# Weight loads of the expert stage from Pool's queue, and the token split on ScalarE and VectorE

## The chip, the cores and the metric

One core of a Trainium2 chip. The time is that of the device, from start to end of one launch, in microseconds (us); of several launches the median is given. The engines of a core run their own instruction lists side by side and meet at semaphores: TensorE (PE: matrix products; PEld is its loading of weights), VectorE (DVE), ScalarE (ACT), GpSimd (POOL) and SyncE (SP). SP, ACT and POOL can also issue DMA transfers; a queue named SPq or POOLq in the profile is the list of such issues on that engine. In this kernel SP issues plain loads and transposes, POOL issues gathers and scatters through lists of row numbers.

## The reference

Three parts follow each other. `x` (8 x 8 x 512 x 64) and a small state attend to each other; the result is laid out as 4352 tokens of 512 numbers. Each token goes to the one of eight experts whose embedding it is nearest to, and the output is a feed-forward layer over all tokens:

```
xread = softmax(x @ state.T) @ state;  sread = softmax(state @ x.T) @ x     # 8 batches, 8 heads
x     = tokens of (xread, sread)                                            # 4352 x 512
e     = argmax(normalized(x) @ normalized(expert_emb).T)                    # one of 8 for each token
out   = gate * (relu(x[e] @ w1[e]) @ w2[e])                                 # w1 512x1024, w2 1024x512
h     = out @ w_in;  y = (max(h, 0) + alpha * min(h, 0)) @ w_out            # w_in 512x2048, w_out 2048x512
```

All in float32. The kernel keeps that precision by splitting each number into two float16 parts, `hi` and `lo`, and adding three products: hi x hi, lo x hi and hi x lo.

## The kernel before, in words

The attention stage takes the first 142 us of the profiled execution, the expert stage goes to about 595 us, and the feed-forward stage (`ffn`) fills the rest. The change lies in the expert stage (`moe`).

The tokens are sorted by expert and cut into tiles of 128, called slots; `step(s)` does the work of one slot. For each slot `mm1` multiplies the tokens by `w1h` and `w1l` (24 products), `relu` splits the result into `hs`, and `mm2` multiplies that by `w2h` and `w2l` (24 products, one slot behind `mm1`: TensorE's order is mm1(s), mm2(s-1), mm1(s+1), mm2(s)). Both need their operand with the tokens along the free axis, so two transfers transpose on the way: `xs` to `xTt` (line 1043) and `hs` to `hT` (line 1060). Both are issued by SP. hT(s) has from the end of the split of mm1(s) to the end of mm1(s+1); xTt(s) is issued two steps ahead.

The tokens of slot s+4 are gathered by Pool (`g_load`, line 1037) into `xg`. Two steps before their use `x_prep` (line 1040) scales them and splits them into `xs`; before, Pool does this in three instructions a slot (`split_pool`, lines 141 to 143). Pool also scatters the finished rows (`y_out`, line 1085), after one small copy (line 1081).

The weights of one expert at a time are in float16 in SBUF. Where the next slot has another expert, `swap` converts the waiting float32 copy (`st1`, `st2`) to float16 on ACT and DVE (`convert`, lines 130, 133, 188) and then loads the next expert's weights into that copy, in four transfers of 512 KB (line 1103). Which slots these are is known only at run time: a table says it, and an engine that takes part reads its flag and branches (lines 1097, 1099, 1107). `sq` squares the loaded copy on ACT (line 164), which gives its scale. An expert's w1 and w2 are changed in neighbouring steps.

In the same steps the feed-forward weights are loaded too, 1 MB at a time (`d_load`, lines 1110 to 1117): 16 of them, one in every second step or so, each decoded by three instructions on DVE (lines 149 to 151) behind it. The first expert's weights are loaded elsewhere, in the attention stage (`w_load`, line 698), from SP; the change leaves that.

What one engine executes is in the order in which the program is written. In one step the order is: mm1, mm2 of the slot before, relu and hT, the change of w1, the feed-forward work left from the step before (with `d_load`), the squares of st2, `x_prep`, `y_top`, the change of w2, the squares of st1, `y_out`, the next gather. A compiler sets the semaphores; an engine that waits holds all that is written behind it.

Of the kernel before, what the change touches and what calls it, by code (L numbers as in the profile page):

```python
# [14 lines left out]
ALU = mybir.AluOpType  # L15
AX = mybir.AxisListType
ET = mybir.EngineType
# [5 lines left out]
def tile_attn_moe_ffn(ctx, tc, x, xt, state, statet, embt, tau, w1, w2, w_in, w_out, alpha, out):  # L23


    nc = tc.nc
    B, S, DM = x.shape
    D, NS = state.shape[2], statet.shape[3]
    H = DM // D
    E, _, FE = w1.shape  # L30
# [84 lines left out]
    def flag(row, s, engines, mx):  # L115
        return nc.values_load(
            tab[0:1, row, s:s + 1], engines=engines, min_val=0, max_val=mx,
            skip_runtime_bounds_check_because="the table is computed in this launch within these bounds",
        )
# [9 lines left out]
    def split_hi(hi, src, sc):  # L129
        nc.scalar.activation(out=hi, in_=src, func=AF.Copy, scale=sc)  # L130

    def split_lo(lo, hi, src, sc):
        nc.vector.scalar_tensor_tensor(out=lo, in0=src, scalar=sc, in1=hi, op0=ALU.mult, op1=ALU.subtract)  # L133

    def split(hi, lo, src, sc):
        split_hi(hi, src, sc)
        split_lo(lo, hi, src, sc)

    def split_pool(hi, lo, src, sc):

        nc.gpsimd.tensor_tensor(src, src, sc.to_broadcast([128, src.shape[1]]), ALU.mult)
        nc.gpsimd.tensor_copy(hi, src)
        nc.gpsimd.tensor_tensor(lo, src, hi, ALU.subtract)

    def decode_ops(dst, d):

# [38 lines left out]
    def convert(i):  # L185
        src, hi, lo = W[i]
        if i == 1:
            nc.vector.tensor_scalar(hi[:, 3, :], src[:, 3, :], a_w[i][:, 0:1], None, ALU.mult)
        for c in range(4):
            if c < 3 or i != 1:  # L190
                split_hi(hi[:, c, :], src[:, c, :], a_w[i])
            split_lo(lo[:, c, :], hi[:, c, :], src[:, c, :], a_w[i])
        nc.vector.reciprocal(inv_w[i], a_w[i])
# [816 lines left out]
    def moe(st, winh, winl, wf, yq, yps, scp, pm, tables, order, gates):  # L1010
# [4 lines left out]
        def ring(pool, n, shape, dt, name):  # L1015
            ts = [pool.tile(shape, dt, name=f"{name}{i}", tag=f"{name}{i}", bufs=1) for i in range(n)]
            return [ts[i % n] for i in range(MS + 1)]

        xg = ring(mp, 5, [128, XW], F32, "xg")
# [19 lines left out]

        def x_prep(s):  # L1040
            xs = xs_[s]
            split_pool(xs[:, 0:DM], xs[:, DM:], xg[s][:, 0:DM], xg[s][:, DM:DM + 1])
            nc.sync.dma_start_transpose(out=xTt[s], in_=xs)

        def mm1(s):
# [50 lines left out]
        def swap(i, s, wv, stg):  # L1096
            with tc.If(flag(0, s, (ET.Activation, ET.DVE), 1) > 0):
                convert(i)
            with tc.If(flag(1, s, (ET.SP,), 1) > 0):
                nxt = flag(2, s, (ET.SP,), E - 1)  # L1100
                n = stg.shape[1] // 4
                for c in range(4):
                    nc.sync.dma_start(stg[:, c * n:(c + 1) * n, :],
                                      wv[bass.ds(nxt, 1), :, c * n:(c + 1) * n, :].rearrange("e p k f -> p (e k) f"))

        def sq(i, s):
            with tc.If(flag(1, s, (ET.Activation,), 1) > 0):
# [2 lines left out]
        def d_load(c):  # L1110
            d64[c] = mp.tile([128, 1024, 2], I32, tag="d64", bufs=1, name="d64")
            if c < 8:
                src = w_in32[(c // 2) * 128:(c // 2 + 1) * 128, (c % 2) * 2048:(c % 2 + 1) * 2048]
                nc.sync.dma_start(d64[c].rearrange("p a b -> p (a b)"), src)
            else:
                src = w_out32[(c - 8) * 256:(c - 7) * 256, :].rearrange("(k p) n -> p k n", p=128)
                nc.sync.dma_start(d64[c].rearrange("p (k a) b -> p k (a b)", k=2), src)

        def d_parts(c):
            cs = slice((c % 8) * 1024, (c % 8 + 1) * 1024)  # L1120
            ops = decode_ops(wf[:, cs], d64[c])
            if c < 15:
                ops.append(lambda: d_load(c + 1))
            return ops
# [6 lines left out]
        d64, work = {}, {s: [] for s in range(MS)}  # L1131
# [20 lines left out]
        x, xs = xg[ES], xs_[ES]  # L1152
        split(xs[:, 0:DM], xs[:, DM:], x[:, 0:DM], x[:, DM:DM + 1])
        nc.sync.dma_start_transpose(out=xTt[ES], in_=xs)
        swap(0, ES, w1v, st1)
        squares(1)
        x_prep(ES + 1)
        order(le, mp, pos, ids)
        for i in range(2):
            nc.gpsimd.memset(ys_[i][:, 2 * DM:YW], 0.0)  # L1160
        y_top(0)
        y_out(0)
        d_load(0)

        left = []

        def step(s):
# [19 lines left out]
            if s + 1 < MS:  # L1187
                swap(0, s + 1, w1v, st1)
# [5 lines left out]
            if s + 2 < MS:  # L1194
                x_prep(s + 2)
            y_top(s - 1)
            swap(1, s, w2v, st2)
            sq(0, s)
            y_out(s - 1, fill)
# [378 lines left out]
```

## Time and profile before

| | |
|---|---|
| three runs | 1281.7, 1278.25, 1269.78 us; median 1278.25 |
| the profiled execution's own time | 1269.9 us |
| its span | 1268.2 us |
| mean granted clock of TensorE | 0.986 |
| busy in the span: PE, DVE, ACT, POOL | 94%, 63%, 45%, 25% |
| chain that ended last | PE 53% of the span, DMA 1%, the others under 0.5% |

The profile is one execution. Its span is cut into stages below; the granted clock is the share of full speed that TensorE was given. In a row of groups the columns are: line, engine, operation, what it writes and reads, shape, count, then busy time in us and the mean of one in ns, then the idle time of the engine just before them and what ended it. A row of waits names the engine and the line that waited, for whom, the total in us, how often, and the longest. A row of a timeline gives the start in us, the duration in us, and in brackets what the engine waited for before.

### The profile page before, as it was taken

The page shows a single profiled execution, that of the slowest core. Times are in us where ns is not written, and L with a number is a line of the kernel's source. Part 1 is how long each engine was busy: PE and PEld are TensorE (multiplying, and loading weights), DVE is VectorE, ACT ScalarE, POOL GpSimd, SP SyncE. Part 2 cuts the span into 40 slices and gives each one's busy share as a digit, 9 for nine tenths or more (in the row PEclk, how much of TensorE's full clock was granted, in tenths as well). Part 3 has the DMA queues.
Part 4 walks back from the last instruction along what each step waited for, and adds up shares of the span by engine and source line. Part 5 has one row for each costly group of instructions (what it writes and reads, how often), then busy time and mean ns, then how long its engine had stood idle before and what let it go on. Part 6 is the DMA issues. An engine that isn't in the chain of part 4 may idle for free.

```text
span 1268.2 us, 21066 instructions
## 1 busy us (share of the span) xinstructions
PE 1194.9 (94%) x7520; PEld 680.0 (54%) x7520; DVE 794.8 (63%) x1648; ACT 565.1 (45%) x1045; POOL 323.3 (25%) x389
## 2 busy tenths in 40 slices
PE   8998899998778899998999999999999999999997
PEld 5555444443333344443446666666666666666664
DVE  5899676586676577755997546445454554555443
ACT  5986422264563545542544334333333433334343
POOL 2113355535345446453202011020100201001010
PEclk9999999998998999998999999999999999999999
DMA  9998678998999999984011010100101002000000
GB/s 286 289 295 257 174 169 203 188 234 202 225 255 209 219 227 234 207 195 88 12 18 51 1 42 26 35 34 1 43 26 34 34 1 51 18 18 35 1 26 26
DMA packets 221648, 148.48 MB, mean 117 GB/s; under 512 B 174014, under 2 KB 190526, under 8 KB 220480
## 3 DMA queue, kind: packets, MB, share of 16 engines
q1 hardware_dynamic: 210976, 117.30, 38.5%
q0 software_dynamic: 10240, 29.49, 8.1%
q8 instruction: 61, 1.00, 0.3%
q14 instruction: 83, 0.68, 0.2%
q10 hardware_dynamic: 288, 0.02, 0.0%
HBM read 80.13 MB, written 28.40 MB: 86 GB/s over the span
## 4 chain that ended last, share of the span: by engine, by line
PE 53%; DMA 1%; DVE 0%; issue 0%; ACT 0%; POOLq 0%; DVEq 0%
PE bk L1394 27%; PE pm L1448 12%; PE bk L1448 9%; PE bk L1410 2%; PE pm L1410 1%; DMA hT<-hs 1%; PE yp L1065 1%; DMA out_dram<-arena,fr 0%; POOLq L1574 0%; DVE ys L133 0%; DVE arena L1454 0%; DVE ym L1072 0%; ACT arena L1399 0%; ACT ys L130 0%; ACT arena L1367 0%
## 5 line engine op out<-in xcount | busy, mean ns | idle before, releaser
L1394 PE MATMUL bk<-woh,arena 128*128 128x512 f16 x1088 | 399.8, 379 | 0.0
L1394 PEld LDWEIGHTS <-arena 128*128 128x128 f16 x1632 | 158.1, 98 | 100.2
L1394 PE MATMUL bk<-wol,arena 128*128 128x512 f16 x544 | 206.2, 379 | 0.0
L1454 DVE SCALAR_TENSOR_TENSOR arena<-bk,sg,arena 128x256 f32<-128x256 f32 (+1 forms) x128 | 59.8, 467 | 215.4 <-PE bk L1448 215.3
L1456 ACT ACTIVATE arena<-pm,sg 128x256 f32<-128x256 f32 (+1 forms) x192 | 88.2, 460 | 195.3 <-PE pm L1448 193.8
L1065 PE MATMUL yp<-w2h,hT 128*128 128x512 f16 x576 | 140.6, 400 | 33.0 <-DMA hT<-hs 32.0
L1065 PEld LDWEIGHTS <-hT 128*128 128x128 f16 x864 | 83.3, 100 | 142.1 <-DMA hT<-hs 39.0
L1367 ACT CAST arena<-arena 128x512 f16<-128x512 f32 (+1 forms) x144 | 85.1, 591 | 157.7 <-DVE arena L1372 156.2
L1052 PEld LDWEIGHTS <-xTt 128*128 128x128 f16 x864 | 84.4, 98 | 122.1 <-DMA xTt<-xs 13.6
L1052 PE MATMUL hp<-w1h,xTt 128*128 128x512 f16 x576 | 133.3, 383 | 15.5 <-DMA xTt<-xs 9.8
L1283 POOL DMA_INDIRECT gt<-gate_d,fr x34 | 36.7, 1078 | 392.7 <-DMA fr<-y_nat 326.3
L1448 PEld LDWEIGHTS <-wS 128*128 128x128 f16 x1152 | 108.3, 98 | 50.6 <-issue 0.2
L1448 PEld LDWEIGHTS <-winh 128*128 128x128 f16 x1024 | 98.6, 98 | 64.5 <-issue 0.8
L1372 DVE SCALAR_TENSOR_TENSOR arena<-arena,alpha_sb 128x512 f32<-128x512 f32 (+1 forms) x144 | 103.0, 716 | 3.2 <-ACT arena L1414 3.2
L1371 DVE TENSOR_TENSOR arena<-arena 128x512 f16<-128x512 f32 (+1 forms) x144 | 94.3, 660 | 16.1 <-ACT arena L1367 13.6
L130 ACT ACTIVATE ys<-yp,ym 128x512 f16<-128x512 f32 x38 | 26.0, 684 | 171.4 <-DVE ym L1074 154.7
L1448 PE MATMUL pm<-ysum,wS 128*128 128x256 f16 (+1 forms) x768 | 99.6, 266 | 0.1
L1085 POOL DMA_INDIRECT y_nat<-ys,pos x38 | 39.4, 1038 | 211.6 <-issue 146.4
L1294 POOL DMA_INDIRECT out_dram<-arena,fr x34 | 34.9, 1025 | 203.9 <-ACT arena L1399 143.7
L1448 PE MATMUL bk<-yT,winh 128*128 128x256 f16 (+1 forms) x512 | 86.5, 266 | 0.0
L1052 PE MATMUL hp<-w1l,xTt 128*128 128x512 f16 x288 | 68.2, 379 | 0.0
L1065 PE MATMUL yp<-w2l,hT 128*128 128x512 f16 x288 | 68.0, 378 | 0.0
(315 smaller groups left out, 1860.5 us busy)
## 6 DMA issues: line engine op xcount, KB each, us to landing
st<-in_w_dram SPq DMA_DIRECT2D x64, 512.0 KB
X<-in_x_dram SPq DMA_DIRECT2D x32, 256.0 KB
d<-in_w_in_dram SPq DMA_DIRECT2D x8, 1024.0 KB
d<-in_w_out_dram SPq DMA_DIRECT2D x8, 1024.0 KB
xs_all<-xrow SPq DMA_DIRECT2D x7, 1056.0 KB
xT<-in_xt_dram SPq DMA_DIRECT2D x7, 1024.0 KB
xs_all<-xrow SPq DMA_DIRECT2D x2, 528.0 KB
xT<-in_xt_dram SPq DMA_DIRECT2D x2, 512.0 KB
```

The source lines that it names most:

```text
L1052: nc.tensor.matmul(hp[s][c], lhsT=xTt[s][:, q + k, :], rhs=wt[:, k, c * 512:(c + 1) * 512], start=(i == 0 and k == 0), stop=(i == 2 and k ...
L1065: nc.tensor.matmul(yp[s], lhsT=hT[s][:, q + k, :], rhs=wt[:, k, :], start=(i == 0 and k == 0), stop=(i == 2 and k == KE - 1))
L1085: nc.gpsimd.indirect_dma_start(out=y_nat[:], out_offset=bass.IndirectOffsetOnAxis(ap=pos[:, s:s + 1], axis=0), in_=ys[:].bitcast(I32), in_ ...
L1283: nc.gpsimd.indirect_dma_start(out=gt[g][:, t:t + 1], out_offset=None, in_=gate_d[:], in_offset=bass.IndirectOffsetOnAxis(ap=fr[g][:, t, 1 ...
L1367: nc.scalar.copy(slot[G[g, m]][:, 0, 0:n], h)
L1371: tt(d[:, 1, 0:n], h, d[:, 0, 0:n], sub)
L1372: return [lambda: nc.vector.scalar_tensor_tensor(h, in0=h, scalar=alpha_sb[:, m:m + 1], in1=h, op0=ALU.mult, op1=ALU.max), hi, lo]
L1394: nc.tensor.matmul(ps, lhsT=slot[G[g, m]][:, lg, t * 128:(t + 1) * 128], rhs=wo[lw][:, m, :], start=(m == order[0] and i == 0), stop=(m == ...
L1410: nc.tensor.matmul(ps, lhsT=wi[l][:, k, m * 128:(m + 1) * 128], rhs=yT[0][:, y + k, :], start=(n == 0), stop=(n == 11))
L1448: nc.tensor.matmul(ps, lhsT=a, rhs=b, start=(i in (1, 2, 5) and j == 0), stop=(j == len(ops) - 1), skip_group_check=True)
L1454: nc.vector.scalar_tensor_tensor(d, in0=ps, scalar=sc, in1=d, op0=ALU.mult, op1=add)
L1456: nc.scalar.activation(out=d, in_=ps, func=AF.Copy, scale=sc)
```

## The change

`split_pool` is gone. `x_prep` calls `split`, the pair that line 130 (ACT) and line 133 (DVE) of the other conversions use. The flag, the branch and the four loads of `swap` move from SP to Pool, and so do the 16 feed-forward loads. Line numbers after the change are 6 lower behind line 143.

```diff
-    def split_pool(hi, lo, src, sc):
-        nc.gpsimd.tensor_tensor(src, src, sc.to_broadcast([128, src.shape[1]]), ALU.mult)
-        nc.gpsimd.tensor_copy(hi, src)
-        nc.gpsimd.tensor_tensor(lo, src, hi, ALU.subtract)
...
         def x_prep(s):
             xs = xs_[s]
-            split_pool(xs[:, 0:DM], xs[:, DM:], xg[s][:, 0:DM], xg[s][:, DM:DM + 1])
+            split(xs[:, 0:DM], xs[:, DM:], xg[s][:, 0:DM], xg[s][:, DM:DM + 1])
             nc.sync.dma_start_transpose(out=xTt[s], in_=xs)
...
-            with tc.If(flag(1, s, (ET.SP,), 1) > 0):
-                nxt = flag(2, s, (ET.SP,), E - 1)
+            with tc.If(flag(1, s, (ET.Pool,), 1) > 0):
+                nxt = flag(2, s, (ET.Pool,), E - 1)
                 n = stg.shape[1] // 4
                 for c in range(4):
-                    nc.sync.dma_start(stg[:, c * n:(c + 1) * n, :],
+                    nc.gpsimd.dma_start(stg[:, c * n:(c + 1) * n, :],
...
-                nc.sync.dma_start(d64[c].rearrange("p a b -> p (a b)"), src)
+                nc.gpsimd.dma_start(d64[c].rearrange("p a b -> p (a b)"), src)
...
-                nc.sync.dma_start(d64[c].rearrange("p (k a) b -> p k (a b)", k=2), src)
+                nc.gpsimd.dma_start(d64[c].rearrange("p (k a) b -> p k (a b)", k=2), src)
```

SP's list in one early step of the expert stage, before: `st` is the float32 copy of expert weights, `tab` the table of flags, `d` a feed-forward load; ISA rows set up the row number of a load.

```order
L1060 DMA_TRANSPOSE hT_2248<-hs_2246 128x16x128
L1092 UNCONDITIONAL_BRANCH
L1097 UNCONDITIONAL_BRANCH
L116 TENSOR_LOAD tab
L1099 COMPARE_AND_BRANCH
L116 TENSOR_LOAD tab
L1103 ISA
L1103 DMA st_122<-in_w_dram 128x1024
...
L1114 DMA d_3331<-in_w_in_dram 128x2048
L1097 UNCONDITIONAL_BRANCH
L1107 UNCONDITIONAL_BRANCH
L1043 DMA_TRANSPOSE xTt_2244<-xs_2242 128x8x128
```

The same part of SP's list after the change:

```order
L1054 DMA_TRANSPOSE hT_2248<-hs_2246 128x16x128
L1086 UNCONDITIONAL_BRANCH
L1091 UNCONDITIONAL_BRANCH
L1093 UNCONDITIONAL_BRANCH
L1101 UNCONDITIONAL_BRANCH
L1037 DMA_TRANSPOSE xTt_2244<-xs_2242 128x8x128
L1091 UNCONDITIONAL_BRANCH
L1093 UNCONDITIONAL_BRANCH
L1101 UNCONDITIONAL_BRANCH
L1054 DMA_TRANSPOSE hT_2249<-hs_2247 128x16x128
```

Between two transposes SP no longer has a flag to read, a load to issue, or a wait that belongs to one.

Pool's list, one step before the change (scatter, gather, split, copy):

```order
L1085 DMA y_nat<-ys_2254,pos 4352x528
L1037 DMA xg_2237<-xs_all,idx 128x528
L141 TENSOR_TENSOR xg_2241<-xg_2241 128x512
L142 CAST xs_2243<-xg_2241 128x512
L143 TENSOR_TENSOR xs_2243<-xg_2241,xs_2243 128x512
L1081 COPY ys_2253<-ids 128x2
```

and after it (of the four loads of one change the first stands):

```order
L1079 DMA y_nat<-ys_2254,pos 4352x528
L1031 DMA xg_2240<-xs_all,idx 128x528
L1086 UNCONDITIONAL_BRANCH
L1091 UNCONDITIONAL_BRANCH
L116 TENSOR_LOAD tab
L1093 COMPARE_AND_BRANCH
L116 TENSOR_LOAD tab
L1097 ISA
L1097 DMA st_122<-in_w_dram 128x1024
...
L1108 DMA d_2877<-in_w_in_dram 128x2048
...
L1075 COPY ys_2253<-ids 128x2
```

The loads now stand between one slot's scatter and gather and the next slot's copy and scatter.

ACT's list after the change, one step: the first half of the token split (`xs<-xg`) stands behind the conversion of w1 and the squares of the other copy.

```order
L191 ACTIVATE hs_2246<-hp_2259 128x512
L1086 UNCONDITIONAL_BRANCH
L116 TENSOR_LOAD tab
L1091 COMPARE_AND_BRANCH
L130 ACTIVATE w1h<-st_122,a_w_105 128x1024 x4
...
L158 ACTIVATE junk,fs<-st_123 128x1024 x4
...
L130 ACTIVATE xs_2242<-xg_2240 128x512
L116 TENSOR_LOAD tab
L1091 COMPARE_AND_BRANCH
L130 ACTIVATE w2h<-st_123,a_w_106 128x1024 x3
```

Before, the list is the same without the row `xs<-xg`; where the flags are not set, the conversions and squares are jumped over.

## Rows read from the trace of the kernel before

**Rows 1.** Stages of the program: stretch, busy us per engine, granted clock, DMA share, GB/s.
```profile
142.00:280.00 138.00, 130.65 (x613) 58.73 (x612) 91.96 (x168) 45.01 (x71) 73.16 (x80) 1.00 0.85 194
280.00:445.00 165.00, 136.09 (x587) 57.86 (x586) 108.28 (x203) 86.14 (x133) 71.19 (x73) 0.94 0.96 222
445.00:595.00 150.00, 134.71 (x617) 58.99 (x616) 101.61 (x185) 72.17 (x105) 73.45 (x76) 0.98 0.84 195
595.00:1268.00 673.00, 666.00 (x4496) 425.69 (x4494) 377.67 (x674) 260.70 (x514) 72.12 (x69) 1.00 0.10 26
```

**Rows 2.** TensorE groups, expert stage: count, busy us, mean ns, idle before, releasers.
```profile
L1065 PE MATMUL yp<-w2h,hT 128*128 128x512 f16 x576 | 140.6, 400 | 33.0 <-DMA hT<-hs 32.0 <-ACTq L1097 0.6 <-DVEq L1097 0.4
...
L1052 PE MATMUL hp<-w1l,xTt 128*128 128x512 f16 x288 | 68.2, 379 | 0.0
```

**Rows 3.** Waits of the expert stage: total us, times, longest.
```profile
PE yp L1065 <- DMA hT<-hs: 32.0, 12, 5.7
...
PE hp L1052 <- DMA xTt<-xs: 9.8, 7, 4.0
```

**Rows 4.** Waits of SP's queue, expert stage: total us, times, longest.
```profile
SPq L1060 <- DMA st<-in_w_dram: 7.4, 5, 2.1
SPq L1043 <- DMA st<-in_w_dram: 7.1, 4, 2.9
```

**Rows 5.** SP's queue in order of time, around an expert change: start us, us.
```profile
394.88 2.55 SPq L1060 DMA_TRANSPOSE hT<-hs  x1
...
403.27 3.50 SPq L1103 DMA_DIRECT2D st<-in_w_dram  x4
409.00 1.27 SPq L1043 DMA_TRANSPOSE xTt<-xs  x1
413.41 1.80 SPq L1060 DMA_TRANSPOSE hT<-hs  x1
```

**Rows 6.** VectorE in order of time: the relu split that the hT of 413.41 moves.
```profile
408.16 0.15 DVE L1059 TENSOR_TENSOR fx<-xg,inv_w 128x1 f32<-128x1 f32 x1
```

**Rows 7.** TensorE: the second product that waited for the hT of 394.88.
```profile
406.47 1.95 PE L1065 MATMUL yp<-w2h,hT 128*128 128x512 f16 x6 [2.93 <-DMA hT<-hs]
```

**Rows 8.** SP's queue in order of time: hT alone, and hT behind d.
```profile
206.90 1.41 SPq L1060 DMA_TRANSPOSE hT<-hs  x1
...
223.29 0.35 SPq L1114 DMA_DIRECT2D d<-in_w_in_dram  x1
...
227.85 3.00 SPq L1060 DMA_TRANSPOSE hT<-hs  x1
```

**Rows 9.** TensorE in order of time: the products those two fed.
```profile
215.36 3.62 PE L1065 MATMUL yp<-w2h,hT 128*128 128x512 f16 x16
...
238.19 3.63 PE L1065 MATMUL yp<-w2h,hT 128*128 128x512 f16 x16 [1.89 <-DMA hT<-hs]
```

**Rows 10.** The chain that ended last: start us, us, what.
```profile
574.49 8.56 DMA hT<-hs
```

**Rows 11.** TensorE: the product that this transpose released.
```profile
583.17 6.09 PE L1065 MATMUL yp<-w2h,hT 128*128 128x512 f16 x16 [5.29 <-DMA hT<-hs]
```

**Rows 12.** Groups of the expert stage, shapes apart: count, busy us, mean ns, idle before.
```profile
L143 POOL TENSOR_TENSOR xs<-xg,xs 128x512 f16<-128x512 f32 x37 | 50.7, 1370 | 3.0
...
L1085 POOL DMA_INDIRECT y_nat<-ys,pos x38 | 39.4, 1038 | 211.6 <-issue 146.4 <-DVE ys L133 32.4 <-DVE hs L198 13.7
L141 POOL TENSOR_TENSOR xg<-xg 128x512 f32<-128x512 f32 x37 | 39.3, 1063 | 3.0 <-DMA xg<-xs_all,idx 2.3
...
L142 POOL CAST xs<-xg 128x512 f16<-128x512 f32 x37 | 33.7, 911 | 2.4
...
L133 DVE SCALAR_TENSOR_TENSOR xs<-xg,xs 128x512 f16<-128x512 f32 x1 | 0.8, 753 | 0.0
L130 ACT ACTIVATE xs<-xg 128x512 f16<-128x512 f32 x1 | 0.7, 721 | 3.9 <-DMA xg<-xs_all,idx 3.9
```

**Rows 13.** VectorE's decoding of d: min, median, max ns.
```profile
L150 DVE SCALAR_TENSOR_TENSOR wf<-d,c_top,wf x16: 1262/1724/2867, 165.7 to 531.6; 128x1024 int32<-128x1024 int32 x16
```

More of the change, by code (lines that the diff above doesn't have):

```diff
@@ L1098, in swap @@
                 convert(i)
-            with tc.If(flag(1, s, (ET.SP,), 1) > 0):
-                nxt = flag(2, s, (ET.SP,), E - 1)
+            with tc.If(flag(1, s, (ET.Pool,), 1) > 0):
+                nxt = flag(2, s, (ET.Pool,), E - 1)
                 n = stg.shape[1] // 4
                 for c in range(4):
-                    nc.sync.dma_start(stg[:, c * n:(c + 1) * n, :],
-                                      wv[bass.ds(nxt, 1), :, c * n:(c + 1) * n, :].rearrange("e p k f -> p (e k) f"))
+                    nc.gpsimd.dma_start(stg[:, c * n:(c + 1) * n, :],
+                                        wv[bass.ds(nxt, 1), :, c * n:(c + 1) * n, :].rearrange("e p k f -> p (e k) f"))
         def sq(i, s):
```

## The prediction, before the result was known

> **What bounds the kernel now.** I began with the cut into stages [rows 1]. The feed-forward stage has TensorE busy for 666.00 of 673 us at full clock; nothing of the change lies there, and it stays. In the expert stage TensorE is busy 130.65 of 138, 136.09 of 165 and 134.71 of 150 us: 51.6 us idle, 28.9 of them in the middle part, where the granted clock is 0.94 and the DMA engines are busy for 0.96 of the time. So the expert stage is nearly bound by TensorE, and short of it by transfers. The groups of TensorE tell which [rows 2]: the second products with w2h, the first to need hT, idle 33.0 us, and one takes 400 ns where the same shape with w1l takes 379. 576 x 21 ns = 12.1 us is thus lost to a lower granted clock just behind these waits. The waits name hT with 32.0 us in 12 stalls and xTt with 9.8 us in 7 [rows 3]. Nothing else stops TensorE for long, so the question is when the two transposes land.
>
> **How late they are, and why.** A transpose undisturbed is in time: one issued at 206.90 [rows 8] fed a product at 215.36 that waited for nothing [rows 9]. The time from issue to need is 8.46 us. The one issued at 227.85, 4.56 us behind a 1 MB load on the same queue [rows 8], fed its product at 238.19 after an idle of 1.89 us [rows 9]: 10.34 us. The one of 394.88 [rows 5] took 11.59 us, to 406.47, with an idle of 2.93 us [rows 7]. A second delay comes before the issue. SP issued four expert loads at 403.27, an xTt at 409.00 and the next hT at 413.41 [rows 5], while the split that this hT moves had ended at 408.16 + 0.15 = 408.31 [rows 6]: SP was 5.1 us late. It was held by waits for weight loads to land: they stand before hT with 7.4 us and before xTt with 7.1 us [rows 4]. Both delays belong to sharing one list and one queue with the weights. The change ends that sharing.
>
> One wait is of another kind. The last hT takes 8.56 us [rows 10] and TensorE idles 5.29 us for it [rows 11], with no weight load left; its 16 products then take 6.09 us, against 3.62 us for the 16 of [rows 9]. These 5.3 + 2.5 us stay.
>
> **The change, part by part.**
>
> *Loads off SP.* Within reach: 32.0 - 5.3 = 26.7 us of hT, 9.8 us of xTt, and 12.1 - 2.5 = 9.6 us of low clock. The best case is all three, 46 us. The worst is below zero, since transposes and weights now compete from two queues (first rival). I take half of hT, -13: some of the late transposes start late because the relu split itself is late in an expert change, behind conversions on ACT and DVE, and this the change doesn't mend. Of xTt I take two thirds, -6, since it is issued two steps ahead and SP is what holds it. Of the clock I take the same half as of hT, -5. Together -24.
>
> *Loads onto Pool.* 48 expert and 16 feed-forward loads. No plain load of Pool stands in these rows; the nearest is its scatter, 1038 ns [rows 12]. At the 0.4 us of SP's load of 403.27 (3.50 us with the waits between the four) [rows 5] it would be 26 us in all, at the scatter's price 64 x 1.04 = 66 us. I take the second, since it is Pool's own. The removed split frees 50.7 + 39.3 + 33.7 = 123.7 us [rows 12], so Pool has 57 us less to do. Pool was busy 217.8 of 453 us [rows 1], and its scatters wait for others (211.6 us of idle before them [rows 12]). Queued behind a waiting load are the copy, the scatter of the slot before and the gather of a slot four ahead; a gather has two steps to spare, a scatter is read only by the feed-forward stage and its early transposes. So this costs nothing, unless the cover ends: a load that waits behind a scatter starts later than it did on SP.
>
> *The token split.* ACT gets 37 x 0.721 = 26.7 us and DVE 37 x 0.753 = 27.9 us [rows 12]. DVE gets some of it back: its decoding line 150 takes 1262 ns at best and 1724 at the median [rows 13], which I put down to Pool's arithmetic running beside it; with that gone, 16 x 0.46 = 7 us come back on that line alone. ACT is busy 203.3 and DVE 301.9 of 453 us [rows 1], so in most slots the 0.7 us fall into idle time. They don't where an expert changes: there the split on ACT stands behind conversions and squares and ahead of the next relu, and each relu that is late already moves by 0.7 us or more. For six changes with two such steps each, 12 x 0.72 = 9 us is the upper bound and 0 the lower; I take +4. In the prologue of the stage the second slot's split now waits behind four squares on ACT: +1.
>
> *Loads late.* A weight that lands later delays its squares, scale and conversion. Nothing to twelve steps by 1 us each; +1 taken.
>
> Sum: -24 + 4 + 1 + 1 = -18, so 1269.9 - 18 = 1252 for an execution like the profiled one. That one lies 8.35 us below the median of the three runs (1278.25), at the low end of them. A median of new runs may lie on either; I put half of the distance on top: **1256 us**.
>
> **The rivals.** *First: the transposes crawl beside the weights (slower).* On one queue the weights were mostly done before the transposes began; on two, both run together for longer, on engines that are busy for 0.96 of the time [rows 1]. Twelve loads of experts (48 / 4) and 16 of feed-forward weights make 28 steps with a load. If hT takes 10.34 us in each, as behind d [rows 8, 9], it is 28 x 1.88 = 53 us of waits against 36.5 paid now: +16, 1286. At the 11.59 us of [rows 5, 7] it is 28 x 3.13 = 88, +51, 1321. Between them I put this case at 1300. It decides from 8.46 + 36.5 / 28 = 9.76 us on. For it: the row of 227.85 has a gather of Pool's queue under way as well. Against it: a transpose now starts at once, not behind a megabyte. Chance 0.14.
>
> *Second: no change.* The same bytes go through the same engines, and the relu split sets hT in the worst slots. Then hT's 26.7 us stay, what SP no longer delays is lost to the slower transfers or to +4 on ACT, and the time is 1270 to 1278. For it: DMA at 0.96; against it: SP's 5.1 us at 408 to 413, which is no matter of bytes. Chance 0.27. The Trainium skill ("DMA: Bandwidth & Descriptors", Issuing engines are not separate DMA queues) says that transfers from all issuing engines run on the same 16 DMA engines and interleave, and that another issuer saves only the time of issuing. By that rule this rival is the forecast. The trace agrees only in part: hT lost 5.1 us of issuing to waits, which is much more than the 0.4 us of a load.
>
> *Third: Pool delivers the loads late (slower).* Pool's list is in order; a load now stands behind a scatter that waits for the end of a slot on DVE, and one issue of Pool's takes 1.04 us [rows 12]. If the loads of 12 changes come 4 us later, and half of that shows at TensorE, that is +24 on the forecast's 1252: 1276; if all of it shows, +48, 1300. As a case of its own, slower than before, I put it at 1293, near the second. It decides where a load's delay passes the slack of its squares. Against it: the scatters take 1038 ns in the mean [rows 12] beside a DVE that is busy two thirds of the time. Chance 0.11. The Trainium skill ("SBUF — State Buffer", the box on the "DVE blocks DMA" trap) warns of this very move: while DVE runs certain fast copies, Pool can't write the descriptors of its transfers, and a transfer from SP or ACT would not wait. No stretch in the mean of the scatters shows it here.
>
> **How the numbers follow.** Forecast 0.48 (1236 to 1268 alone), no change 0.27, the two slower rivals 0.25. A difference of less than 1% (1265 to 1291) can't be told from none here. The forecast at its upper edge falls within 1%, and a mild third rival too; the two make up for each other. So faster 0.48, same 0.28, slower 0.24. The range goes from 1230, most of the best case's 46 us, to 1292, which leaves out the worse half of the slower rivals.
>
> **What would show it.** In the profile after: SP's waits for weight loads gone, and hT issued within 0.1 us of the split's end; waits of TensorE for hT at about 19 us and for xTt at about 4; the mean of the w2h products at about 390 ns; line 150 near 1.3 us; Pool's plain loads near 1 us; ACT's relu in the changes 0.7 us later. I am wrong if hT takes over 9.8 us from issue to landing in the steps with loads, if squares wait for `st` much longer than before, or if TensorE's idle time stays at 50 us with the waits under other names.

## The result, and the profile after

The changed kernel takes 1284.08 us (median of 20 runs), the kernel before 1273.01 us in 20 runs beside it: ratio 1.0092, interval 1.0068 to 1.0115. This ratio, like all below, leaves out executions in a slower state, here 2 of the 20. It is slower by 0.9%, where I had forecast faster. The profiled execution has a span of 1286.6 us, 18.4 us over the one before.

All of that lies in the expert stage, which now ends at about 609 us and not at 591. Its cut, as in [rows 1] (stretch, busy us of PE, PEld, DVE, ACT, POOL, granted clock, DMA share, GB/s):

```profile
142.00:280.00 138.00, 128.69 (x590) 57.31 (x588) 84.23 (x175) 49.45 (x79) 30.82 (x48) 0.98 0.76 186
280.00:445.00 165.00, 131.88 (x564) 55.95 (x564) 102.37 (x198) 96.74 (x146) 50.78 (x68) 0.91 0.90 216
445.00:610.00 165.00, 143.20 (x640) 62.56 (x641) 109.50 (x207) 82.27 (x121) 45.46 (x63) 0.95 0.86 188
```

Pool is busy for 50.78 us in the middle stretch, 71.19 before; TensorE is busy 4.2 us less there, and its granted clock fell from 0.94 to 0.91. TensorE's two groups that wait, of which the first answers to [rows 2]; the third row is the second group before the change:

```profile
L1059 PE MATMUL yp<-w2h,hT 128*128 128x512 f16 x576 | 141.2, 401 | 31.5 <-DMA hT<-hs 29.5 <-ACTq L1091 1.2 <-DVEq L1091 0.8
L1046 PE MATMUL hp<-w1h,xTt 128*128 128x512 f16 x576 | 137.6, 392 | 27.9 <-DMA xTt<-xs 21.9 <-ACT w1h L130 3.5 <-ACTq L1091 1.7
...
L1052 PE MATMUL hp<-w1h,xTt 128*128 128x512 f16 x576 | 133.3, 383 | 15.5 <-DMA xTt<-xs 9.8 <-ACT w1h L130 2.6 <-ACTq L1097 2.5
```

Over all groups of the stage TensorE's idle time goes from 48.5 to 61.5 us, and the two groups above are busy 4.9 us longer, the one with w1h 4.3 of them. That is nearly all of the 18.4 us.

The waits, as in [rows 3], with ScalarE's for weights:

```profile
PE yp L1059 <- DMA hT<-hs: 29.5, 9, 6.6
...
ACT w2h L130 <- DMA st<-in_w_dram: 22.3, 5, 8.1
PE hp L1046 <- DMA xTt<-xs: 21.9, 7, 12.9
...
ACT junk L158 <- DMA st<-in_w_dram: 15.0, 12, 6.7
```

hT still costs 29.5 us (32.0 before), xTt 21.9 (9.8 before): the loss is xTt's. What the change removed, it did remove: in one slot the relu split ends at 404.87 + 1.29 = 406.16 and its hT is issued at 406.19 (start us, us):

```profile
404.87 1.29 DVE L192 SCALAR_TENSOR_TENSOR hs<-hp,hs 128x512 f16<-128x512 f32 x2 [0.77 <-ACT hs L191]
...
406.19 2.14 SPq L1054 DMA_TRANSPOSE hT<-hs  x1
```

Over the 36 slots hT is issued 1.0 us in all behind the end of its split, 18.6 us before. VectorE's decoding, 1724 ns at the median in [rows 13], is no longer stretched:

```profile
L144 DVE SCALAR_TENSOR_TENSOR wf<-d,c_top,wf x16: 1266/1285/1286, 169.5 to 544.9; 128x1024 int32<-128x1024 int32 x16
```

So SP's list is free and VectorE is faster, and the transposes land no sooner after their issue. By the records of their landing hT takes 6.8 us in the mean (6.7 before) and at most 14.3 (11.5), xTt 5.7 us (5.0) and at most 17.9 (8.1). Two places stand out. The first is the first feed-forward load. Before, it was issued at 151.48 and the first hT, at 158.07, fed a product at 162.48 without a wait:

```profile
151.48 0.36 SPq L1114 DMA_DIRECT2D d<-in_w_in_dram  x1
...
158.07 1.66 SPq L1060 DMA_TRANSPOSE hT<-hs  x1
...
162.48 3.62 PE L1065 MATMUL yp<-w2h,hT 128*128 128x512 f16 x16
```

Now it stands behind a scatter:

```profile
157.71 1.04 POOL L1079 DMA_INDIRECT y_nat<-ys,pos  x1 [3.04 <-DVE ys L133]
...
158.76 0.61 POOL L1108 DMA_DIRECT2D d<-in_w_in_dram  x1
...
159.04 1.43 SPq L1054 DMA_TRANSPOSE hT<-hs  x1
...
167.44 0.82 PE L1059 MATMUL yp<-w2h,hT 128*128 128x512 f16 x3 [3.83 <-DMA hT<-hs]
```

The load is issued 7.3 us later, 0.3 us ahead of hT, and TensorE waits 3.83 us. The DMA engines in the four microseconds from 160 (GB/s in 40 slices, then packets, MB and share by queue; q0 is Pool's, q1 SP's):

```profile
GB/s 42 0 0 0 82 655 328 82 82 246 166 84 0 84 82 82 164 0 3 251 164 169 335 248 422 504 87 422 422 251 509 586 84 338 174 755 256 169 676 335
...
q0 software_dynamic: 128, 0.91, 86.3%
q1 hardware_dynamic: 81, 0.02, 2.3%
```

Both queues had work, and of SP's transposes (packets of 256 bytes) 81 got through, 0.02 MB. From 166 to 167, alone, they moved 1152. The second place is an expert change:

```profile
364.79 0.75 POOL L1111 DMA_DIRECT2D d<-in_w_out_dram  x1 [0.28 <-issue]
...
365.47 1.23 SPq L1175 DMA_TRANSPOSE y<-y_nat  x1
...
366.81 4.51 SPq L1037 DMA_TRANSPOSE xTt<-xs  x1
...
368.23 0.73 POOL L1097 DMA_DIRECT2D st<-in_w_dram  x1 [2.69 <-ACT junk L158]
...
369.42 0.71 POOL L1097 DMA_DIRECT2D st<-in_w_dram  x1 [0.46 <-ACT junk L158]
...
370.61 0.71 POOL L1097 DMA_DIRECT2D st<-in_w_dram  x1 [0.48 <-issue]
...
371.49 0.71 POOL L1097 DMA_DIRECT2D st<-in_w_dram  x1 [0.17 <-DVE inv_w L187]
...
373.14 10.05 SPq L1054 DMA_TRANSPOSE hT<-hs  x1
...
384.79 1.46 PE L1046 MATMUL hp<-w1h,xTt 128*128 128x512 f16 x3 [12.95 <-DMA xTt<-xs]
```

1 MB of feed-forward weights and 2 MB of w2 are issued on Pool within 7 us, and an xTt of 256 KB, issued 2 us behind the first, is ready 18.0 us later. (Ahead of it in SP's queue is `y`, a transpose of finished rows for the feed-forward stage.) TensorE idles 12.95 us. A transfer reports its landing in 16 parts: 15 of this xTt's came by 380.82 us, the last at 384.74. For some of that time next to nothing moves in either queue; the GB/s from 374 to 378 us, 44 in the mean:

```profile
GB/s 0 46 0 44 0 44 0 44 3 41 44 0 166 0 44 5 123 371 0 125 0 44 44 0 44 0 44 44 0 46 0 44 0 44 44 0 44 123 44 44
```

### The profile page after: what moved, and what is told of

Read it like the earlier page. It is cut to its first block, busy times and chain, and to the rows that moved or that the text cites. A ratio compares the mean times of both kernels' runs of the same rounds, so it can differ in the third digit from the quotient of the medians.

```text
span 1286.6 us, 20929 instructions
## 1 busy us (share of the span) xinstructions
PE 1199.6 (93%) x7520; PEld 681.4 (53%) x7520; DVE 791.8 (62%) x1685; ACT 591.2 (46%) x1082; POOL 230.2 (18%) x342
## 3 DMA queue, kind: packets, MB, share of 16 engines
q0 software_dynamic: 20480, 71.44, 17.4%
## 4 chain that ended last, share of the span: by engine, by line
PE 54%; DMA 2%; issue 0%; DVE 0%; ACT 0%; POOLq 0%; DVEq 0%
PE bk L1388 27%; PE pm L1442 12%; PE bk L1442 9%; PE yp L1059 2%; PE bk L1404 2%; DMA hT<-hs 1%; PE pm L1404 1%; PE hp L1046 1%; DMA out_dram<-arena,fr 0%; POOLq L1568 0%; DVE ys L133 0%; DVE arena L1448 0%; DVE ym L1066 0%; ACT arena L1393 0%; ACT ys L130 0%
## 5 line engine op out<-in xcount | busy, mean ns | idle before, releaser
L1059 PE MATMUL yp<-w2h,hT 128*128 128x512 f16 x576 | 141.2, 401 | 31.5 <-DMA hT<-hs 29.5
L1046 PE MATMUL hp<-w1h,xTt 128*128 128x512 f16 x576 | 137.6, 392 | 27.9 <-DMA xTt<-xs 21.9
L1277 POOL DMA_INDIRECT gt<-gate_d,fr x34 | 33.8, 995 | 390.3 <-DMA fr<-y_nat 325.1
L1288 POOL DMA_INDIRECT out_dram<-arena,fr x34 | 34.6, 1018 | 209.4 <-ACT arena L1393 136.3
L192 DVE SCALAR_TENSOR_TENSOR hs<-hp,hs 128x512 f16<-128x512 f32 x72 | 46.2, 683 | 36.8 <-ACT hs L191 36.8
L158 ACT ACTIVATE junk<-st 128x1024 bf16<-128x1024 f32 x56 | 59.1, 1056 | 20.3 <-DMA st<-in_w_dram 15.0
```

The lines of the kernel that those rows point to most:

```text
L158: nc.scalar.activation(out=junk, in_=W[i][0][:, c, :], func=AF.Square, accum_out=fsq[i][:, c:c + 1])
L192: nc.vector.scalar_tensor_tensor(hs[:, 1, cs], in0=h, scalar=0.0, in1=hs[:, 0, cs], op0=ALU.max, op1=ALU.subtract)
L1046: nc.tensor.matmul(hp[s][c], lhsT=xTt[s][:, q + k, :], rhs=wt[:, k, c * 512:(c + 1) * 512], start=(i == 0 and k == 0), stop=(i == 2 and k ...
L1059: nc.tensor.matmul(yp[s], lhsT=hT[s][:, q + k, :], rhs=wt[:, k, :], start=(i == 0 and k == 0), stop=(i == 2 and k == KE - 1))
```

## The experiments

They are told in the order in which they were run. Theory Q: transposes that run beside loads on another queue are held by them. Theory S: the token split makes xs and relu late. Theory P: Pool's list holds scatters and gathers, and loads come late. Each ratio is to the kernel before in runs on the same chip, with its 95% interval.

**Each part alone.** e1 has the split of the change and both loads on SP; e2 has the loads on Pool and the old split.

```diff
 e1, from the change: swap and d_load use (ET.SP,) and nc.sync again
 e2, from the kernel before: swap and d_load use (ET.Pool,) and nc.gpsimd
```

> The change without its queue part: both kinds of load go back to SP, the token split stays on ScalarE and VectorE. Theory Q (the loss is the second queue: transposes that run beside large packets of Pool's queue get one small packet in for each large one): the loss is gone and VectorE's gain from a quiet Pool shows, ratio to the kernel before 0.994 to 1.002, waits of TensorE for xTt back to about 10 us (22 with the whole change). Theory S (the loss is the split, which makes xs and the relu late): ratio 1.006 to 1.012, waits as with the whole change. Theory P (the loads come late because Pool's list holds them): as Q here.

> The queue part alone: all 64 loads on Pool, the token split stays on Pool too. Theory Q: ratio 1.007 to 1.015, TensorE waits 25 us or more for hT and about 20 for xTt. Theory S: 0.990 to 1.002. Theory P: the worst of all, 1.012 to 1.03, since the loads stand behind 3.3 us of arithmetic per slot as well; ScalarE's waits for st over the 37 us of the whole change (22.3 for the conversion of w2, 15.0 for the squares).

e1: 0.9933 (0.9907 to 0.996), e2: 1.0167 (1.0129 to 1.0206). Theory S has fallen. The product of the two, 1.0099, is the change's 1.0092: the two halves have opposite signs. But e2 is not the loads' half with a free list. Pool's split now stands behind the loads, SP's xTt waits for it, and hT behind that xTt is issued 20.5 us late in all (18.6 before the change):

```profile
SPq L1043 <- POOL xs L143: 94.9, 15, 10.8
```

e2's ratio lies above Q's range and in P's, and so do ScalarE's waits for weights, 46.5 us. With SP's list free the loads on Pool cost 1.6%, the change against e1. In e1 TensorE's waits for hT fall to 19.6 us (second row), though hT is issued 14.1 us late in all:

```profile
L1046 PE MATMUL hp<-w1h,xTt 128*128 128x512 f16 x576 | 137.5, 391 | 16.8 <-DMA xTt<-xs 12.0 <-ACT w1h L130 3.1 <-ACTq L1091 1.1
L1059 PE MATMUL yp<-w2h,hT 128*128 128x512 f16 x576 | 135.8, 390 | 22.7 <-DMA hT<-hs 19.6 <-DVEq L1091 1.8 <-ACTq L1091 1.2
```

**One kind of load on Pool.**

```diff
 e3, from the change: d_load uses nc.sync again (expert loads stay on Pool)
 e4, from the change: swap uses (ET.SP,) and nc.sync again (d_load stays on Pool)
```

> The whole change but for the 16 feed-forward loads, which go back to SP: 25 MB on Pool's queue, 17 MB on SP's. Theory Q: the first stage (142 to 280 us, where only feed-forward loads run) as before, the middle as with the whole change; ratio 1.002 to 1.008. Theory P: the same or a little better than the whole change, since an expert load's landing is what Pool waits on; 1.006 to 1.010. Theory S: 1.009.

> The whole change but for the 48 expert loads, which go back to SP: 17 MB on Pool's queue. Theory Q: ratio 1.000 to 1.006, with an hT of the first two slots late as in the whole change (a stall of 4 us behind the first 1 MB load). Theory P: 0.995 to 1.002, since ScalarE's waits for st are gone. Theory S: 1.009.

e3: 0.9977 (0.9949 to 1.0005), e4: 0.9986 (0.9948 to 1.0025). Against e1 each kind costs 0.4 to 0.5%, both together 1.6%. The intervals are too wide to show that this is more than the sum. Both ratios lie below what Q asked for, and e4's in P's range. In e3 no wait for xTt is longer than 2.3 us:

```profile
PE hp L1046 <- DMA xTt<-xs: 8.8, 5, 2.3
```

**Smaller pieces, and their control.** Each load becomes two transfers (four for the second half of the feed-forward weights): every second kilobyte in e5, 64 partitions each in e8.

```diff
+                    for h in range(2):     # e5: every second kilobyte, for st and d64 alike
+                        nc.gpsimd.dma_start(stg[..].rearrange("p k (i j f) -> p k i j f", j=2, f=256)[:, :, :, h, :], ...)
+                    for h in (slice(0, 64), slice(64, 128)):     # e8
+                        nc.gpsimd.dma_start(stg[h, c * n:(c + 1) * n, :], ...)
```

> The whole change, but every load goes out as two to four transfers whose contiguous pieces are 1 KB (each transfer takes every second kilobyte); 144 issues on Pool in place of 64. Theory Q (packets of the two queues take turns one by one, so a transpose moves one 256 byte packet for each packet of the load): with packets of a quarter to an eighth the size a transpose beside a load gets through several times faster; ratio to the kernel before 0.995 to 1.004, TensorE's waits for hT and xTt under 40 us together (51 with the whole change). Theory P (Pool's list holds the loads and what is behind them): 80 more issues make it worse, 1.010 to 1.020.

> The control to the run with 1 KB pieces: the whole change, and every load as two to four transfers again (144 issues), but each of 64 partitions, so that the pieces stay as long as they were (2 to 8 KB). Theory Q: no gain, ratio 1.008 to 1.018. Theory P: 1.010 to 1.020, the same as the run with 1 KB pieces.

e5: 1.1006 (1.0949 to 1.1062), e8: 1.1583 (1.1529 to 1.1636). Neither theory had a price like these. e5 did not test what it was for: its count of packets on Pool's queue is 22784, with the whole change 20480, so pieces of 1 KB did not become packets of 1 KB. Q's sign in the waits did come, 25.4 us for hT and xTt together, and the time got longer all the same. What both show is that the same bytes in more transfers of Pool's are dear. The loads land later still; in e5 the conversion of w2 waits for them for 69.0 us, 22.3 with the whole change:

```profile
ACT w2h L130 <- DMA st<-in_w_dram: 69.0, 5, 15.8
```

In a stretch of e8 a load keeps the transposes out. From 329 to 336 us, with an xTt issued at 330.56 waiting:

```profile
DMA packets 489, 1.51 MB, mean 215 GB/s; under 512 B 121, under 2 KB 121, under 8 KB 489
...
q0 software_dynamic: 464, 1.51, 104.7%
q1 hardware_dynamic: 25, 0.00, 0.4%
```

**xTt ahead of the feed-forward load, on SP; and a busy Pool.** e6 moves `x_prep` up. e7 is e1 with Pool's old arithmetic into tiles that nobody reads.

```diff
 e6, from e1, in step():
+            if s + 2 < MS:
+                x_prep(s + 2)
             while left: ...
             if s > ES: sq(1, s - 1)
-            if s + 2 < MS:
-                x_prep(s + 2)
 e7, from e1, in x_prep() behind split(...):
+            nc.gpsimd.tensor_tensor(dum, xg[s][:, 0:DM], xg[s][:, DM:DM + 1].to_broadcast([128, DM]), ALU.mult)
+            nc.gpsimd.tensor_copy(dumh, dum)
+            nc.gpsimd.tensor_tensor(dumh, dum, dumh, ALU.subtract)
```

> The split on ScalarE and VectorE, all loads on SP, and in each step the token split and its xTt stand ahead of the feed-forward work and its 1 MB load. By theory Q what is ahead in one queue decides: an xTt ahead of d lands sooner, hT behind it is not worse; ratio 0.986 to 0.993 (the split alone gave 0.9933), TensorE's wait for xTt from 12 us to under 8. If xTt is off the path: 0.993.

> The split on ScalarE and VectorE, all loads on SP, and Pool still does the three instructions of the old split, into tiles that nobody reads. Theory V (the split alone gains 0.7% because Pool is quiet: VectorE's instructions are no longer stretched and Pool's scatters and gathers are not queued behind arithmetic): ratio 0.998 to 1.004, VectorE's line with c_top back to a median over 1.6 us. Theory W (the gain comes from the place of the split, xs being ready earlier): 0.993.

e6: 0.9933 (0.9908 to 0.9958): xTt's wait fell to 5.8 us as expected, and the time did not. xTt is not what bounds e1. e7: 1.0066 (1.0039 to 1.0092): Pool's arithmetic, which nobody reads, costs 1.3% against e1. Theory W falls. Theory V has the direction and not the numbers: the time lies above its range, and the median of the line with c_top is 1337 ns, not over 1.6 us. The longest show the stretch; e1 has maxima of 1348 and 1322 ns for these two lines (min, median, max):

```profile
L144 DVE SCALAR_TENSOR_TENSOR wf<-d,c_top,wf x16: 1256/1337/2821, 169.3 to 535.3; 128x1024 int32<-128x1024 int32 x16
L145 DVE SCALAR_TENSOR_TENSOR wf<-d,c_sh,wf x16: 1283/1512/2065, 172.1 to 536.6; 128x1024 int32<-128x1024 int32 x16
```

TensorE's waits under VectorE's name, the conversion of w2 and what stands behind it, are longer (e1: 1.8 and 0.2 us):

```profile
PE yp L1064 <- DVEq L1096: 8.3, 9, 2.8
PE yp L1064 <- DVE w2l L133: 8.0, 4, 6.4
```

Of the second row 6.4 us are put down wrongly: they are the wait for the last hT, which landed at 590.31 us, just ahead of the product at 590.42, and which e1 has too (5.75 us).

The Trainium skill ("SBUF — State Buffer", SBUF: two separate sides) says that a GpSimd operation that reads SBUF and a VectorE operation with two inputs in SBUF take turns at a port pair, each for a whole instruction. The two decoding lines have two such inputs, and their maxima, 2821 and 2065 ns against 1348 and 1322, agree. Line 143, with one input, was stretched too, from 697 to 2105 ns at most; whether for the same reason no run shows.

**Which queue.** The 16 feed-forward loads alone, at one place in the step, from SP (e11, the reference), ScalarE (e9) and Pool (e10). e12 has xTt right behind hT, all loads on SP.

```diff
 e9 to e11, from e6, in step(); the loads are collected in dl
             if s > ES: sq(1, s - 1)
+            while dl:
+                d_load(dl.pop(0))     # nc.sync in e11, nc.scalar in e9, nc.gpsimd in e10
 e12, from e1: x_prep(s + 2) stands ahead of swap(0, s + 1, w1v, st1)
```

> Token split on ScalarE and VectorE; in each step xTt first, then the feed-forward decoding, then the squares, then the 1 MB feed-forward load; all loads on SP. It is the reference for the next two, which differ from it in the queue of the 16 feed-forward loads alone. Expected by both theories: as the split alone, ratio 0.988 to 0.995.

> As the reference, but the 16 feed-forward loads are issued from ScalarE's queue: a second queue of the kind that SP has, and nothing of Pool's list. Theory Q in its general form (any second queue of large packets slows the transposes): 0.4 to 0.8% above the reference, TensorE's waits for hT and xTt up by 5 to 10 us. Theory Q' (only Pool's queue does so) and theory P (Pool's list): as the reference, within 0.3%.

> As the reference, but the 16 feed-forward loads are issued from Pool's queue. Theories Q and Q': 0.4 to 0.8% above the reference, with transposes that overlap a load getting almost nothing through until it is done. Theory P: 0.2 to 0.8% above it, with TensorE's added waits under ScalarE's or VectorE's names (tokens that came late) and not under the transposes'.

> The split on ScalarE and VectorE, all loads on SP, and the token split and its xTt stand right behind hT, ahead of the change of w1 and its four loads too. If what stands ahead of a transpose in SP's one queue costs time, the 12 us that TensorE waits for xTt shrink to under 4 and the ratio goes under 0.990; if the conversion of w1, now 0.7 us later, decides, it goes over 0.995.

e11: 0.9936 (0.99 to 0.9971), e10: 1.0 (0.9967 to 1.0034), e9: 1.0082 (1.0046 to 1.0117). With nothing else changed, Pool's queue costs 0.64% for 16 loads, and the waits for hT grow, as Q has it (the first row is e10, the second e11):

```profile
PE yp L1059 <- DMA hT<-hs: 29.7, 12, 7.7
...
PE yp L1059 <- DMA hT<-hs: 22.0, 8, 7.1
```

But slow transposes are only a part of it. Pool issues the first load 8.3 us later, and 4.1 us of e10's waits are there. And hT is issued 20.7 us late in all, 13.1 in e11, behind expert loads of SP's that land 6.2 us after their issue in place of 5.7; from its own issue hT takes 6.6 us in the mean, 6.3 in e11. The Trainium skill ("DMA: Bandwidth & Descriptors", Issuing engines are not separate DMA queues) would have it that another issuer changes the time of issuing alone; by that e10 should be no slower than e11, its median is 8.6 us longer, and the measurement decides. e9 doesn't tell Q from Q': ScalarE itself was held (4.6 us in this row for e11), which I had not priced:

```profile
ACT ys L130 <- ACTq L1101: 78.8, 15, 13.3
```

e12: 1.0026 (0.9995 to 1.0056). xTt's waits are gone from the list, and hT's rise to 34.6 us in its place (it is issued 23.8 us late in all, e1 14.1): here what goes first in the one queue is paid by what goes behind.

**A held list, and loads behind hT.** In e13 the loads are on SP and Pool reads one word of each quarter of `st` behind every change. In e14 (whole change) and e15 (e10) Pool reads one word of hT before the loads, the first feed-forward load among them.

```diff
 e13, from e1:  +  nc.gpsimd.tensor_copy(dum[:, c:c + 1], stg[:, c * n, 0:1])     # c = 0..3, behind swap
 e14, e15:      +  nc.gpsimd.tensor_copy(dum[:, 0:1], hT[s][:, 0, 0:1])            # ahead of swap(0, ..), d_load
```

> The split on ScalarE and VectorE, all loads on SP (as in the run with the split alone, 0.9933), and Pool reads one word per partition of each quarter of st behind every change of weights, so that its list is held until the four expert loads have landed, as it is with the loads on Pool. Theory P: ratio 1.003 to 1.012. Theory Q: 0.992 to 0.998 (8 tiny copies in each slot are about 1 us of Pool, which is idle then).

> The whole change, and in each step Pool reads one word per partition of hT before it goes on to the loads: no load of the step starts before this hT has landed; the first feed-forward load, too, comes behind the first hT. Theory Q: better than the whole change (1.0092), 0.997 to 1.005, and TensorE's waits for hT under 20 us (29.5). Theory P: loads start later still, 1.012 to 1.025.

> As the run with the 16 feed-forward loads late and on Pool's queue (1.0000; 0.9936 with them on SP), and Pool waits for this step's hT to land before each of them. Theory Q: most of the 0.64% comes back, 0.993 to 0.997, with no stall of the first hT behind the first load (4.3 us). Theory P: 1.000 or above.

e13: 0.9958 (0.9931 to 0.9986). Pool waited for weights to land, and against e1 it cost 0.25%, less than the intervals can tell from none:

```profile
POOL dum L1104 <- DMA st<-in_w_dram: 97.4, 39, 7.8
```

P asked for 1.003 at least, so the holding of scatters and gathers isn't the cost. e13 also shows what a late issue is worth. Its hT is issued 24.6 us late in all, more than before the change, and TensorE waits 6.5 us for it by name, 10.3 with a wait that is put down to ScalarE:

```profile
PE yp L1060 <- DMA hT<-hs: 6.5, 4, 4.2
```

e14: 1.0411 (1.0356 to 1.0467), e15: 1.0018 (0.9986 to 1.005): Q was wrong that keeping loads away from hT helps. The first hT of e15 no longer stalls, but the load that waited for it is missing elsewhere, and VectorE waits for it ahead of the next relu:

```profile
DVE wf L143 <- DMA d<-in_w_in_dram: 7.2, 1, 7.2
```

In these runs a load from Pool had no good time: early it kept a transpose out, late it kept VectorE and, in e14, ScalarE (51.0 us of waits for st in the conversion of w2).

**The places.** e16 puts the first feed-forward load ahead of the first scatter, e17 the token split ahead of the squares, e18 both; all from the whole change.

```diff
 e16, e18:   +        d_load(0)
                      y_top(0)
                      y_out(0)
             -        d_load(0)
 e17, e18:   x_prep(s + 2) moved as in e6
```

> The whole change, with the first feed-forward load ahead of the first slot's scatter in Pool's list. Theory F (the first load, 7.3 us late behind a scatter, runs into the first hT): the stall of 4.0 us and its slow products (1.7 us) go, ratio to the kernel before 1.003 to 1.007 (1.0092 with the whole change). Otherwise 1.008 to 1.011.

> The whole change, with the token split and xTt ahead of the feed-forward work and the squares of st2. Theory L (loads from Pool land later, ScalarE waits for them in the squares, and the token split behind these is late): TensorE's wait for xTt from 22 us to under 10, ratio 1.000 to 1.005. Theory Q (the transposes themselves crawl): 1.006 to 1.011, waits as before. With the loads on SP the same move changed nothing (0.9933 both times).

> Both moves on the whole change. If F and L are the whole of the queue's cost: 0.993 to 0.998, as with the loads on SP. If a part is left to the second queue itself: 0.999 to 1.006.

e16: 1.0052 (1.0011 to 1.0094), e17: 1.0066 (1.0028 to 1.0103), e18: 1.0041 (1.0004 to 1.0079). The first load may be worth about 0.4 of the 1.6%, but e16's interval overlaps the whole change's, so theory F is not decided. In e17 xTt's wait seems to fall to 9.2 us, as theory L asked; but the second place is only under another name:

```profile
PE hp L1046 <- DMA xTt<-xs: 9.2, 4, 4.8
PE hp L1046 <- ACT junk L158: 8.4, 1, 8.4
```

The xTt issued at 363.68 landed at 377.56 us, and the product that idled 8.4 us started at 377.61. So TensorE waited 17.6 us for xTt, and waits and time are those that Q named. e18 stays 1.1% above e6, which has the same order of the split and its loads on SP. And in e18 the second place is there again, in the same slot: d, then `y` and xTt, 1.4 us behind it, w2 behind both, and the product 20.8 us after its xTt:

```profile
362.63 0.75 POOL L1111 DMA_DIRECT2D d<-in_w_out_dram  x1 [0.92 <-DVE ym L1066]
...
364.03 3.34 SPq L1037 DMA_TRANSPOSE xTt<-xs  x1
...
384.82 1.46 PE L1046 MATMUL hp<-w1h,xTt 128*128 128x512 f16 x3 [15.27 <-DMA xTt<-xs]
```

The change, e16, e17 and e18 all have this place: TensorE idles 12.95, 17.55, 8.4 and 15.27 us there. In e3, e4 and e10, where only one of the two kinds of load is on Pool, no wait for xTt passes 2.3 us. Nor has e2 the place: its xTt of that slot was issued at 374.26 us, when d had all but landed (374.97), and TensorE waits 2.3 us. So the place needs both kinds and an xTt between them, and it doesn't explain e2, which has 27.4 us of waits for xTt in ten places, 9.4 us the longest.

## Why the prediction was wrong, point by point

**What bounds the kernel** held: everything happened in the expert stage, most of it by TensorE waiting for transposes.

**Loads off SP, the term of -24 us, is the step that failed.** It said that the delays "belong to sharing one list and one queue with the weights", and counted half of hT's waits, two thirds of xTt's and half of the clock's loss as gained. The list was freed as foretold (18.6 us of late issues went to 1.0), and that was worth nothing that the runs show: e1 has hT 14.1 us late and e13 24.6, and both are faster than the kernel before. And the second queue is no way past the weights: with the list free the loads on Pool cost 1.6%, 20 us (the change against e1), in place of -24. Most wrong of its three parts is xTt's: +12.1 us where I took -6; hT's waits gave 2.5 us and not 13, and the products with w1h, which the term left out, took 4.3 us more. hT came to 29.5 us of waits (I wrote about 19), xTt to 21.9 (about 4), the products with w2h to a mean of 401 ns (390).

**The first rival** came nearest, but not in its form. It spread the damage over 28 steps of hT and put 1300 us on it; in the trace it is two places above all, at 3.8 and 12.95 us of idle TensorE, and the longer is xTt's. My sign for it, hT over 9.8 us from issue to landing, came in three steps, and before the change in six. So its lower price, 1286, is near the measured 1284 by luck, and the range held the result only because it was widened for the slower rivals. At 0.14 it was too low: the 10.34 us of [rows 8, 9], with a gather of Pool's queue under way, stood for it, and I followed it no further.

**Loads onto Pool** cost less to issue than taken: 637 ns each for the expert loads, not the scatter's 1038, and Pool had room. The clause that I put beside it, a load behind a scatter starts later than on SP, decided the first load.

**The token split** was priced at +4 and +1 and measured -0.67%, or -8.5 us. The 7 us of VectorE that I worked out were named and not entered in the sum. e7 gives both halves: the work on ScalarE and VectorE, with Pool as busy as before, costs 0.66% (8.4 us, my upper bound was 9), and a quiet Pool gives back 1.3%, about 17 us. By the small cost of e13's held list the stretch of VectorE is the likelier reason; no run took it apart. I took a stretch of an engine that is busy for two thirds of the time to lie beside other work; in an expert change it lies ahead of the relu.

**Loads late** was +1. From issue to landing the 48 expert loads took 5.5 us in the mean before and 7.1 after, at most 8.7 and 13.4. ScalarE's waits for them came to 37.3 us; before, they were 6.5 us under the loads' name and 17.2 under that of SP's flag (line 1099). How much of this third rival reaches TensorE no run separates from the crawl.

**What stays open**: why both queues crawl for microseconds, at 44 GB/s, when a transpose meets loads of Pool's. In the second place it isn't VectorE, which is idle from 376.1 to 386.7 us. That this place is most of the loss is argued from its size and its recurrence; no run took it away alone. Whether the size of the packets matters is open too, since it could not be varied. And e2 loses as much without the place.

The best of these kernels are the split alone (e1) and the same with xTt ahead (e6), both 0.9933: the half of the change that I had counted as a cost.

## What to carry to other kernels

Before a transfer is moved to another queue, look in the trace for a moment in which the two queues already run together, and follow what happens there before a gain is entered. Freeing a list gains only what its late issues cost the bottleneck; here that was nothing to be seen. When a wait moves to another name, compare the landing of each transfer with the start that it could have held. When an engine is emptied, look at the minimum and the median of its neighbours' instructions: the difference is what its quiet gives back, and it counts most where that neighbour stands ahead of the bottleneck. Split a change that does two things into its halves before it is judged; here one half gained 0.7% and the other, on top of it, lost 1.6%.

## What the runs showed of the hardware

- Three elementwise operations a slot on Pool, into tiles that nobody reads, cost 1.3% of the kernel; one VectorE operation beside them took up to 2821 ns, at most 1348 without them.
- SP's transposes, in packets of 256 bytes, moved 81 packets in 4 us beside a 1 MB load of Pool's queue; alone 1152 in one.
- Of the 16 parts in which a transfer reports its landing, one came 3.9 us behind the other 15, and TensorE waited for it.
- The same weights in twice as many transfers from Pool made the kernel 10% slower (every second kilobyte) and 16% slower (64 partitions each).
